# Regrouping the matrix work of a tuned attention and MLP block by tile mode, with a head that uses one PSUM bank per transposed chunk

## The chip, the cores and the metric

The kernel runs on one core of a Trainium2 chip. The metric is device time in microseconds (us) of one execution; less is better. "Span" is the length of the profiled execution, about 1.7 us less than the device time of the same run. A DMA is issued by an engine's queue and "lands" when its data have arrived. Engines: PE (matmul), DVE (vector), ACT (activation), POOL (GpSimd) and SP, which here only issues DMAs.

## The reference, cut to what matters

Sequence 2048, width 448, 16 heads of width 28, hidden width 1792; everything in bf16.

```python
xn = layernorm(x)
q, k, v = split(xn @ wqkv)                    # linear attention, phi(t) = t+1 or exp(t)
s = (phi(q) @ (phi(k).T @ v)) / (phi(q) @ sum(phi(k))) @ wo
g = silu(relu(xn @ w1 + b1)**2 @ w2 + b2)     # the gate
return x + s * g
```

The kernel splits the sequence into 16 tiles of 128 tokens. Its names for the stages are used below: H (xn @ w1, in groups of 512 tokens), K and Q, "q-rest" (the last 64 columns of q), token sum (xn.T @ phi(k)), den and spread (the denominator), gate (the product with w2, one per tile), S (phi(q) times the folded matrix). A tile's result is S x gate (a DVE instruction that reads S from PSUM), plus x (an "add", on POOL or DVE), and then one store.

Of the kernel before, what the change touches and what calls it, by code (L numbers as in the profile page):

```python
# [9 lines left out]
P = 128  # L10
# [5 lines left out]
NGB, NOB = 8, 6  # L16
# [12 lines left out]
class Op:  # L29
    def __init__(self, eng, emit, reads, writes, dur, alts, nbytes):  # L30
        self.eng, self.emit, self.dur, self.alts, self.nbytes = eng, emit, dur, alts, nbytes
        self.reads, self.writes = list(reads), list(writes)
        self.raw, self.deps, self.succ = set(), set(), []
        self.start = self.end = None
        self.seq = None
        self.late = 1e9
        self.prio = None
        self.sync = None
        self.fence = False
        self.fixed = 0.0  # L40
        self.hold = ()
        self.rank = None


class Program:
# [42 lines left out]
    def schedule(self):  # L88
# [26 lines left out]
        free["pool"] = 0.8  # L115
        dma_free = 0.0
# [31 lines left out]
        while n:  # L148
            best = None
            for e in self.ENGINES:  # L150
                if e in fixed:
# [17 lines left out]
                    cand = (st, 0, op, e, banks, op.dur)  # L169
# [37 lines left out]
            st, _, op, e, banks, du = best  # L207
            if op.eng != e:
                pend[op.eng].remove(op)
                op.eng = e  # L210
            else:
                pend[e].remove(op)
# [82 lines left out]
def bass_recurrent_scan__linear_attn_block__dense_activation_squared_relu__prompt_kernel(  # L295
    nc, A_x, A_wqkv, A_wo, B_x, B_w1, B_b1, B_w2, B_b2, out
):
    with ExitStack() as es:
# [205 lines left out]
        def pe_four(a, b, c, d, close=True, part=None, need=()):  # L504
# [10 lines left out]
            for lo, hi, us in ((0, 4, (a, c)), (4, 8, (b, d)), (8, 11, (c, a)), (11, 14, (d, b))):  # L515
# [18 lines left out]
                )  # L534
                ops.append(op)
# [6 lines left out]
        def pe_two(a, b, close=True):  # L542
            lo, hi, full = slice(0, 64), slice(64, 128), slice(0, 128)

            def f(e, _):
                for u in (a, b):
                    for k in range(3):
                        u[2](e, full, k, k == 0, False)
                a[2](e, lo, 3, False, close)
                return b[2](e, hi, 3, False, close)  # L550

            add("pe", f, a[1] + [r for r in b[1] if r not in a[1]], [a[0], b[0]], 7 * MM(a[4]) + 0.1)
            if close:
                a[3]()
                b[3]()

        def pe_main(u):
# [7 lines left out]
            add("pe", f, u[1], [u[0]], 3 * MM(u[4]) + 0.03)  # L565
# [16 lines left out]
        def pe_tails(a, b, close=True, need=()):  # L582
# [4 lines left out]
            op = add("pe", f, a[1] + [r for r in b[1] if r not in a[1]] + list(need) + [a[0], b[0]], [a[0], b[0]], MM(a[4]) + 0.1)  # L587
# [62 lines left out]
        def qx(u):  # L650
# [20 lines left out]
            add("pe", f, xnames(2 * u) + xnames(2 * u + 1) + wnames("wq") + ["wqh"], [b], 4 * MM(512) + 0.1)  # L671
# [45 lines left out]
        def dup(lo, hi, act=False):  # L717
            if act:
                add(
                    "act",  # L720
                    lambda e, _: e.activation(out=xn[:, lo:hi, D:512], in_=xn[:, lo:hi, 384:D], func=AF.Copy),
                    [("xn", k) for k in range(lo, hi)], [("xnd", k) for k in range(lo, hi)], 0.2,
                )
                return
            add(
                "dve", lambda e, _: e.tensor_copy(xn[:, lo:hi, D:512], xn[:, lo:hi, 384:D]),
                [("xn", k) for k in range(lo, hi)], [("xnd", k) for k in range(lo, hi)], 0.12,
            )

        def x_transpose0(lo, between=None):  # L730
            bs = [Buf("T"), Buf("T"), None, Buf("T")] if lo == 0 else [Buf("T")] * 4
            bs[2] = bs[0]

            def piece(cs, tail):
                def f(e, _):
                    last = None
                    for c in cs:
                        v = ps(bs[c])[:, :].bitcast(bf)
                        for k in (0, 1):
# [5 lines left out]
                    "pe", f, [(("xnd" if tail else "xn"), lo + k) for k in (0, 1)] + ["ident"],  # L745
                    list(dict.fromkeys(bs[c] for c in cs)), len(cs) * 0.114,
                )

            if lo == 0:
                piece((0, 1, 2), False)  # L750
                piece((3,), True)
            else:
                piece((0, 1, 2, 3), True)
            src = lambda c0, c1: (
                ps(bs[c0])[:, :].bitcast(bf)[:, c0 * 256 : c1 * 256].rearrange("p (c k t) -> p c k t", c=c1 - c0, k=2)
            )
            dst = lambda c0, c1: xT[:, lo : lo + 2, c0:c1, :].rearrange("p k c t -> p c k t")

            def on_act(c):
                return add(  # L760
                    "act", lambda e, _: e.activation(out=dst(c, c + 1), in_=src(c, c + 1), func=AF.Copy),
                    [bs[c]], [("xTp", lo, c)], 0.39,
                )

            def on_dve(c0, c1):
                return add(
                    "dve", lambda e, _: e.tensor_copy(dst(c0, c1), src(c0, c1)), [bs[c0]],
                    [("xTp", lo, c) for c in range(c0, c1)], 0.1 + 0.16 * (c1 - c0),
                )

            if lo == 0:
                on_act(0)
                on_dve(1, 2)
                on_act(2)
                between()
                return on_act(3)
            on_dve(0, 1)
            on_dve(1, 2)
            return on_dve(2, 4)

# [9 lines left out]
        def token_sum(c):  # L790
            b = Buf("A")

            def f(e, _):
# [14 lines left out]
            add(  # L808
                "pe", f, [(n, i) for n in ("pk", "xn") for i in range(NT)], [b], (16 if c < 3 else 8) * MM(D) + 0.1
            )  # L810
# [53 lines left out]
        def fold_wo(c):  # L864
# [15 lines left out]
            add("pe", f, ["kvd", "kvm", "wo"], [b], 0.19 * len(hs) + 0.05)  # L880
# [10 lines left out]
        def den():  # L891
            def f(e, _):
# [21 lines left out]
                [denb], 4 * 0.24,  # L914
            )
# [10 lines left out]
        def spread(c):  # L926
# [19 lines left out]
            add("pe", f, ["rden", "ehd"], bufs, 0.3)  # L946
# [69 lines left out]
        def gate(si, b, lo, hi, k, final):  # L1016
# [5 lines left out]
                "dve", lambda e, _: e.tensor_tensor(out=ob, in0=ps(b)[:, 0:w], in1=gs, op=ALU.mult),  # L1022
# [24 lines left out]

        def ss2(t, final=()):
            pe_two(*(sunit(si, si in final) for si in (t, t + 1)))

        def s_tails(parts):
# [4 lines left out]
            def f(e, _):  # L1056
                last = None
                for si, lo, hi, b in us:
                    r = slice(64 * (si % 2), 64 * (si % 2) + 64)
                    last = e.matmul(  # L1060
                        ps(b)[:, 0 : hi - lo], pqx[r, si // 8, (si % 8) // 2, :], msb[r, 3, lo:hi], start=True, stop=False
# [3 lines left out]
            add("pe", f, [("pqy", 3), ("msb", 3)], [u[3] for u in us], 0.2 * (len(us) // 2))  # L1065
            return us

        def s_main(u, k, final=True):
            si, lo, hi, b = u
            w = hi - lo  # L1070

            def f(e, _):
                last = None
                for c in range(3):
                    last = e.matmul(  # L1075
                        ps(b)[:, 0:w], pqT[:, c, si * P : (si + 1) * P], msb[:, c, lo:hi], start=False, stop=(c == 2)
# [39 lines left out]
        warm(40, 0.107)  # L1116
# [6 lines left out]
        dup(0, 1)  # L1123
        ln_rstd(1, 2)
        bias_columns()
        ln_norm(1)
        dup(1, 2, True)
        ln_stats(2)
        x_transpose0(0, lambda: ln_rstd(2, 3))
# [3 lines left out]
        dup(2, 3)  # L1133
        ln_norm(3)
        dup(3, 4)
        warm(4, 0.056)
# [3 lines left out]
        t23 = x_transpose0(2)  # L1140
# [27 lines left out]
        qx(0)  # L1168
        gg(0)
        gg(1)  # L1170
        ln(12, 16, lead=2)
# [3 lines left out]
        gg(2)  # L1175
        gg(3)
# [5 lines left out]
        quads("Q2.0 H3.4 Q2.1 H3.6 Q2.2 H3.5 Q3.0 H3.7 Q3.1 H3.12 Q3.2 H3.13")  # L1182
        qx(1)
        token_sum(0)
# [4 lines left out]
        token_sum(3)  # L1189
# [17 lines left out]
        ggs(6)  # L1207
        spread(3)
        ggs(7)
        ss4(0)  # L1210
        ggs(8)
        ggs(9)
        ss4(1)
        for si in range(10, 13):
            ggs(si)
        ss4(2)
        ggs(13)
        ggs(14)
        us = s_tails([(12, 0, D), (13, 0, D), (14, 0, D), (15, 0, 224), (15, 224, D)])
        for k in range(3):  # L1220
            s_main(us[k], k)
        gg_part(15, 0, 224)
        s_main(us[3], 3)
        gg_part(15, 224, D)
        s_main(us[4], 4)
# [30 lines left out]
```

## The kernel before: the parts that the change touches

448 is 3 x 128 + 64. A contraction over 448 is three full-array matmuls and one that fills only half of PE's rows; two such halves run side by side. A tile mode is the way in which PE's array is divided: used whole, or as row or column parts that work side by side; going from one to another is called a mode switch here. H, K, Q and S are written in a 64-row tile mode (two row halves at once), except for part of the first H work and the main part of the last S tiles, which use the full array; the gates use the full array; q-rests and the fourth token sum use a 64-column mode; spread uses a 32-row mode. PE writes its results to PSUM, which has eight banks. The main program is a list of such stages; a list scheduler in the kernel puts the instructions of the other engines in order, while PE keeps the order of the list.

```python
def x_transpose0(lo, between=None):           # head: tiles 0 and 1
    bs = [Buf("T"), Buf("T"), None, Buf("T")] if lo == 0 else [Buf("T")] * 4
    bs[2] = bs[0]                             # chunks 0 and 2 share a PSUM bank
    ...
    if lo == 0:
        piece((0, 1, 2), False)               # six transposes in one instruction group
        piece((3,), True)
    ...
# main program, cut
        quads("Q0.2 H1.12 Q1.0 H1.13"); qx(0); gg(0); gg(1)
        quads("K2.0 H2.0 ... H2.7"); gg(2); gg(3)
        ...
        qx(1); token_sum(0); token_sum(1); z_cols(); token_sum(2); den(); token_sum(3)
        quads("H3.8 H3.9 H3.10 H3.11")
        ...
        ggs(6); spread(3); ggs(7)
        ss4(0); ggs(8); ggs(9); ss4(1)
        for si in range(10, 13): ggs(si)
        ss4(2); ggs(13); ggs(14)
        us = s_tails([(12, 0, D), (13, 0, D), (14, 0, D), (15, 0, 224), (15, 224, D)])
        for k in range(3): s_main(us[k], k)   # adds of tiles 12, 13, 14 on DVE
        gg_part(15, 0, 224); s_main(us[3], 3)
        gg_part(15, 224, D); s_main(us[4], 4)
```

(`ss4(i)` is the S group of tiles 4i to 4i+3; its four adds run on POOL. Cuts are marked with dots; several calls are put on one line here.)

## Time and profile before

| | before |
|---|---|
| device time, median | 147.02 us (3 runs), 146.99 us in the 6 runs of the comparison |
| span of the profiled run | 145.4 us |
| PE busy | 141.2 us, 97% of the span |
| first H matmul | 6.81 us |
| last DVE add ends | 143.37 us (143.09 + 0.28) |
| last store issued | 143.39 us |

The page of the kernel before. The first line is the span, the second the busy time per engine with the number of instructions, the third the shares of the chain of waits, which is the chain of work that ended last:

```profile
span 145.4 us, 2861 instructions
...
PE 141.2 (97%) x1139; PEld 72.3 (50%) x1139; DVE 96.1 (66%) x219; ACT 79.5 (55%) x153; POOL 35.3 (24%) x51
...
PE 96%; DVE 1%; ACT 1%; issue 0%
```

PE is the bound: 96% of the chain is PE, and other engines' idle time costs nothing.

The chain of waits before, in order of time (start us, length us, what). L705 is the first H work, L709 H, L657 q-rest 0, L970 gates:

```profile
6.29 0.39 ACT xT L761
6.68 0.12 issue
6.81 2.12 PE pb L705 x18
...
11.79 1.09 PE pb L705 x9
...
14.82 0.86 PE pb L709 x8
...
37.49 0.98 PE pb L657 x8
38.47 5.40 PE pb L970 x28
...
96.29 2.65 PE pb L970 x14
...
100.82 2.75 PE pb L970 x14
...
143.09 0.28 DVE obuf L1028
```

A gate is 14 matmuls. After full-array work it takes 2.65 us; after another tile mode it takes 2.75 us. The first number gives 0.189 us for one matmul, so 28 should take 5.30 us and take 5.40. This 0.1 us per change of mode is what the change goes after.

The DMA view before, for the stretch in which the first 512 columns of w1 are issued (2.20 us); the last column is us from issue to landing:

```profile
w<-in_B_w_dram SPq DMA_DIRECT2D x1, 384.0 KB, 4.5
```

It lands at about 2.20 + 4.5 = 6.7 us, just when the copy (ACT, ends at 6.68) is done.

The end of the kernel before: from its timeline, POOL's adds for S group 2 and DVE's adds for tiles 12 to 14 (start us, us, engine, line, operation, count), and then SP's last two store issues, each asked for by itself:

```profile
132.08 4.00 POOL L1028 TENSOR_TENSOR obuf<-obuf,x_tok 128x448 bf16<-128x448 bf16 x4 [7.33 <-DVE obuf L1022]
...
139.65 0.98 DVE L1028 TENSOR_TENSOR obuf<-obuf,x_tok 128x448 bf16<-128x448 bf16 x3
...
141.66 0.33 SPq L401 DMA_DIRECT2D out_dram<-obuf  x1
...
143.39 0.33 SPq L401 DMA_DIRECT2D out_dram<-obuf  x1
```

POOL is done at 136.1 us, seven microseconds before the end. The last store is issued at 143.39 us, 0.02 us after its add.

### The profile page before, as it was taken

To read this page: it belongs to the slowest core of one execution; us is meant where nothing else is said; L and a number is where in the kernel's file an instruction comes from. 1 tells how busy PE (TensorE), PEld (TensorE's weight loads), DVE (VectorE), ACT (ScalarE), POOL (GpSimd) and SP (SyncE) were. 2 spreads that over 40 slices of the span, in tenths; PEclk is the share of its full clock that TensorE was granted. 3 is DMA by queue.
4 is the path that set the end of the run, shared out by engine and by line. 5 is a ranking of instruction groups with operands and counts; after the bars stand their busy time and mean duration, and the time that the engine had idled before them with its cause. 6 is when DMAs were issued, how large, how long until landed. Compare 5 with 4: busy or idle time off the path is not lost.

```text
span 145.4 us, 2861 instructions
## 1 busy us (share of the span) xinstructions
PE 141.2 (97%) x1139; PEld 72.3 (50%) x1139; DVE 96.1 (66%) x219; ACT 79.5 (55%) x153; POOL 35.3 (24%) x51
## 2 busy tenths in 40 slices
PE   7999999999999999999999999999999999999992
PEld 7884444444444444444443554454444544544481
DVE  6979888799987995278999500079683516216281
ACT  3627897988886981388879713897311110310300
POOL 2013026470000551630560000000000907306400
PEclk9999999999999999999999999999999999999999
DMA  4967699943301400000000000000000220200312
GB/s 90 316 231 227 146 247 371 330 110 72 77 0 34 111 5 0 0 0 5 0 2 0 5 0 0 0 2 5 0 0 0 66 65 32 95 0 5 126 62 64
DMA packets 16025, 10.53 MB, mean 72 GB/s; under 512 B 7500, under 2 KB 15628, under 8 KB 16012
## 3 DMA queue, kind: packets, MB, share of 16 engines
q1 hardware_dynamic: 15824, 10.28, 25.0%
q8 instruction: 9, 0.15, 0.4%
q10 hardware_dynamic: 188, 0.07, 0.2%
q14 instruction: 4, 0.03, 0.1%
HBM read 6.94 MB, written 1.84 MB: 60 GB/s over the span
## 4 chain that ended last, share of the span: by engine, by line
PE 96%; DVE 1%; ACT 1%; issue 0%
PE pb L970 28%; PE pb L709 26%; PE pb L617 7%; PE pb L797 6%; PE pb L643 6%; PE pb L1039 6%; PE pb L705 3%; PE pb L1089 3%; PE pb L992 2%; PE pb L1075 1%; PE pb L657 1%; PE pb L803 1%; PE pb L874 1%; PE pb L741 1%; PE pb L934 1%; PE pb L826 1%
## 5 line engine op out<-in xcount | busy, mean ns | idle before, releaser
L970 PE MATMUL pb<-w,r 128*128 128x448 bf16 x210 | 41.3, 353 | 0.0
L676 ACT ACTIVATE r<-pb,b1f 128x512 bf16<-128x512 f32 x54 | 33.8, 691 | 10.6 <-PE pb L709 10.6
L709 PE MATMUL pb<-xT,w 64*128 64x512 bf16 (+1 forms) x291 | 38.5, 376 | 0.0
L970 PEld LDWEIGHTS pb<-w,r 128*128 128x128 bf16 x210 | 19.8, 98 | 20.0 <-issue 1.5
L1012 ACT ACTIVATE gbuf<-gbuf 128x448 bf16<-128x448 bf16 x15 | 8.5, 581 | 29.7 <-DVE gbuf L979 29.7
L1028 POOL TENSOR_TENSOR obuf<-obuf,x_tok 128x448 bf16<-128x448 bf16 x12 | 12.0, 1032 | 48.6 <-DVE obuf L1022 48.6
L709 PEld LDWEIGHTS pb<-xT,w 64*128 64x128 bf16 (+1 forms) x291 | 14.1, 94 | 16.6 <-issue 0.4
L627 POOL TENSOR_TENSOR zacc<-zacc,pk 128x448 f32<-128x448 f32 x13 | 14.6, 1126 | 31.4 <-DVE pk L607 28.0
L979 DVE TENSOR_TENSOR gbuf<-pb,b2b 128x448 bf16<-128x448 f32 x15 | 9.4, 623 | 16.5 <-PE pb L970 16.4
L690 DVE TENSOR_TENSOR r<-r 128x512 bf16<-128x512 bf16 x35 | 16.8, 518 | 2.8 <-ACT r L676 2.7
L1022 DVE TENSOR_TENSOR obuf<-pb,gbuf 128x448 bf16<-128x448 f32 (+1 forms) x17 | 9.2, 592 | 6.6 <-PE pb L1039 4.7
L957 DVE TENSOR_TENSOR pqT<-pqT,pb 128x512 bf16<-128x512 bf16 x12 | 7.4, 681 | 8.8 <-PE pb L934 8.8
L617 PE MATMUL pb<-w_qkv,xT 64*128 64x448 bf16 x112 | 13.2, 349 | 0.0
L691 ACT ACTIVATE r<-r 128x512 bf16<-128x512 bf16 x21 | 12.6, 635 | 0.0
L643 PE MATMUL pb<-xT,w_qkv 64*128 64x512 bf16 x84 | 11.0, 376 | 0.0
L709 PE MATMUL pb<-xT,w_1r 64*128 64x512 bf16 x56 | 10.3, 377 | 0.0
L607 DVE SCALAR_TENSOR_TENSOR pk<-pb,pk 128x448 bf16<-128x448 f32 x16 | 9.9, 623 | 0.5
L461 DVE BATCH_NORM_STATS2 st<-x_tok 128x6 f32<-128x448 bf16 x16 | 9.2, 613 | 1.2 <-DMA x_tok<-in_A_x_dram 1.1
L595 ACT ACTIVATE pk<-pb 128x448 bf16<-128x448 f32 x16 | 7.8, 541 | 3.9 <-PE pb L617 3.9
L797 PE MATMUL pb<-pk,xn 128*128 128x448 bf16 x48 | 9.4, 353 | 0.0
L617 PEld LDWEIGHTS pb<-w_qkv,xT 64*128 64x128 bf16 x112 | 5.4, 94 | 6.1 <-issue 0.4
L607 DVE SCALAR_TENSOR_TENSOR pqT<-pb,pqT 128x512 bf16<-128x512 f32 x12 | 8.2, 690 | 0.3
(92 smaller groups left out, 133.7 us busy)
## 6 DMA issues: line engine op xcount, KB each, us to landing
out_dram<-obuf SPq DMA_DIRECT2D x15, 112.0 KB, 1.8
w<-in_B_w_dram SPq DMA_DIRECT2D x1, 1568.0 KB, 9.3
x_tok<-in_A_x_dram SPq DMA_DIRECT2D x3, 448.0 KB, 4.0
w<-in_B_w_dram SPq DMA_DIRECT2D x3, 384.0 KB, 4.5
w_qkv<-in_A_wqkv_dram SPq DMA_DIRECT2D x3, 336.0 KB, 5.7
w_o<-in_A_wo_dram SPq DMA_DIRECT2D x1, 392.0 KB, 9.1
w_qkv<-in_A_wqkv_dram SPq DMA_DIRECT2D x6, 56.0 KB, 5.2
x_tok<-in_A_x_dram SPq DMA_DIRECT2D x2, 112.0 KB, 2.1
```

Source lines behind the costliest of these rows:

```text
L607: lambda e, _: e.scalar_tensor_tensor(out=slot, in0=ps(buf)[:, 0:n], scalar=1.0 + 1e-6, in1=slot, op0=ALU.add, op1=ALU.max),
L617: return e.matmul(ps(b)[:, 0:D], xT[rw, si, c, :], w_qkv[rw, c, D : 2 * D], start=start, stop=stop)
L627: lambda e, _: e.tensor_tensor(out=o[:, 0:D], in0=pk[:, 0, :] if i == 1 else zacc[:, :], in1=pk[:, i, :], op=ALU.add),
L643: return e.matmul(ps(b)[:, 0:512], w_qkv[rw, c, m * P : (m + 1) * P], xT[rw, 4 * g : 4 * g + 4, c, :], start=start, stop=stop,)
L676: rl = lambda e, _: e.activation(out=slot, in_=ps(b)[:, 0:512], func=AF.Relu, bias=b1f[:, fi : fi + 1])
L690: return e.tensor_tensor(out=slot, in0=slot, in1=slot, op=ALU.mult)
L691: return e.activation(out=slot, in_=slot, func=AF.Square)
L709: return e.matmul(ps(b)[:, 0:512], lhs, xT[rw, 4 * g : 4 * g + 4, c, :], start=start, stop=stop, skip_group_check=not full,)
L797: last = e.matmul(ps(b)[:, 0:D], xn[:, si, c * P : (c + 1) * P], pk[:, si, :], start=(si == 0), stop=(si == NT - 1),)
L970: last = e.matmul(ps(b)[:, 0:D], r2[:, fi, si * P : (si + 1) * P], w_2[:, fi, :], start=(fi == 0), stop=(fi == NF - 1),)
L979: lambda e, _: e.tensor_tensor(out=gbuf[:, si % NGB, :], in0=ps(b)[:, 0:D], in1=b2b[:, :], op=ALU.add),
L1028: lambda e, _: e.tensor_tensor(out=ob, in0=ob, in1=x_tok[:, si, lo:hi], op=ALU.add),
```

## The change

The intent: put stages of the same tile mode next to each other, so that PE changes its mode less often; start H earlier with a PSUM bank per transposed chunk and with small copies moved to POOL. The core of the diff, cut:

```diff
-NGB, NOB = 8, 6
+NGB, NOB = 8, 8
 # head
-        def x_transpose0(lo, between=None):
-            bs = [Buf("T"), Buf("T"), None, Buf("T")] if lo == 0 else [Buf("T")] * 4
+        def x_transpose0(lo, pieces, share=()):
 ...
-        dup(0, 1)
+        dup(0, 1, "pool")
 ...
+        piece, evac = x_transpose0(0, [(0,), (1,), (2,), (3,)])
+        for c in range(4):
+            piece((c,))
+        evac("act", 0, 1)
 ...
 # middle
-        qx(0)
         gg(0)
         gg(1)
+        gg(2)
+        gg(3)
 ...
-        gg(2)
-        gg(3)
 ...
+        qx(0)
         qx(1)
+        token_sum(3)
         token_sum(0)
 ...
-        token_sum(3)
 # tail
         ggs(6)
+        ggs(7)
         spread(3)
-        ggs(7)
-        ss4(0)
-        ggs(8)
-        ggs(9)
+        ss4_rests_last(0)
         ss4(1)
-        for si in range(10, 13):
+        for si in range(8, 15):
             ggs(si)
         ss4(2)
-        ggs(13)
-        ggs(14)
-        us = s_tails([(12, 0, D), (13, 0, D), (14, 0, D), (15, 0, 224), (15, 224, D)])
+        us = s_tails([(12, 0, D), (13, 0, D), (14, 0, D), (15, 0, D)])
         for k in range(3):
-            s_main(us[k], k)
+            s_main(us[k], k, k > 0)
```

(The last line moves the add of tile 12 from DVE to POOL. `ss4_rests_last` is a new order inside S group 0 that leaves the half-array matmuls to the end. The cuts also leave out the scheduler's new cost of a mode switch.)

More of the change, by code (lines that the diff above doesn't have):

```diff
@@ L42, in __init__ @@
         self.rank = None
+        self.mode = "full"
 class Program:
@@ L115, in schedule @@
         free["pool"] = 0.8
+        mode = "full"
         dma_free = 0.0
@@ L168, in schedule @@
                     st = max(r, free[e])
-                    cand = (st, 0, op, e, banks, op.dur)
+                    switch = 0.1 if e == "pe" and op.mode != mode else 0.0
+                    cand = (st, 0, op, e, banks, op.dur + switch)
                 else:
@@ L207, in schedule @@
             st, _, op, e, banks, du = best
+            if e == "pe":
+                mode = op.mode
             if op.eng != e:
@@ L534, in pe_four @@
                 )
+                op.mode = "row64"
                 ops.append(op)
@@ L550, in f @@
                 return b[2](e, hi, 3, False, close)
-            add("pe", f, a[1] + [r for r in b[1] if r not in a[1]], [a[0], b[0]], 7 * MM(a[4]) + 0.1)
+            add("pe", f, a[1] + [r for r in b[1] if r not in a[1]], [a[0], b[0]], 7 * MM(a[4]) + 0.2)
             if close:
@@ L563, in f @@
                 return last
-            add("pe", f, u[1], [u[0]], 3 * MM(u[4]) + 0.03)
+            add("pe", f, u[1], [u[0]], 3 * MM(u[4]))
         def pe_part(us, part, cs=(0, 1, 2)):
@@ L585, in f @@
                 return b[2](e, slice(64, 128), 3, False, close)
-            op = add("pe", f, a[1] + [r for r in b[1] if r not in a[1]] + list(need) + [a[0], b[0]], [a[0], b[0]], MM(a[4]) + 0.1)
+            op = add("pe", f, a[1] + [r for r in b[1] if r not in a[1]] + list(need) + [a[0], b[0]], [a[0], b[0]], MM(a[4]))
+            op.mode = "row64"
             if close:
@@ L670, in qx @@
                 )
-            add("pe", f, xnames(2 * u) + xnames(2 * u + 1) + wnames("wq") + ["wqh"], [b], 4 * MM(512) + 0.1)
+            add("pe", f, xnames(2 * u) + xnames(2 * u + 1) + wnames("wq") + ["wqh"], [b], 4 * MM(512)).mode = "col64"
             phi(b, pqx[:, u, :, :].rearrange("p a b -> p (a b)"), ("pqx", u), 512)
@@ L715, in hh, with dup, piece @@
             return b, reads + w1names(fi // 4), mm, lambda: h_out(b, g, fi), 512
-        def dup(lo, hi, act=False):
-            if act:
-                add(
-                    "act",
-                    lambda e, _: e.activation(out=xn[:, lo:hi, D:512], in_=xn[:, lo:hi, 384:D], func=AF.Copy),
-                    [("xn", k) for k in range(lo, hi)], [("xnd", k) for k in range(lo, hi)], 0.2,
-                )
-                return
-            add(
-                "dve", lambda e, _: e.tensor_copy(xn[:, lo:hi, D:512], xn[:, lo:hi, 384:D]),
-                [("xn", k) for k in range(lo, hi)], [("xnd", k) for k in range(lo, hi)], 0.12,
-            )
-        def x_transpose0(lo, between=None):
-            bs = [Buf("T"), Buf("T"), None, Buf("T")] if lo == 0 else [Buf("T")] * 4
-            bs[2] = bs[0]
-            def piece(cs, tail):
+        def dup(lo, hi, eng="dve"):
+            add(
+                eng, lambda e, _: e.tensor_copy(xn[:, lo:hi, D:512], xn[:, lo:hi, 384:D]),
+                [("xn", k) for k in range(lo, hi)], [("xnd", k) for k in range(lo, hi)], 0.25 if eng == "pool" else 0.18,
+            )
+        def x_transpose0(lo, pieces, share=()):
+            bs = [None] * 4
+            for p in pieces:
+                b = Buf("T")
+                for c in p:
+                    bs[c] = b
+            for c, o in share:
+                bs[c] = bs[o]
+            def piece(cs, ks=(0, 1)):
                 def f(e, _):
@@ L738, in f @@
                         v = ps(bs[c])[:, :].bitcast(bf)
-                        for k in (0, 1):
+                        for k in ks:
                             o = (c * 2 + k) * P
@@ L744, in piece, with evac, f @@
                 add(
-                    "pe", f, [(("xnd" if tail else "xn"), lo + k) for k in (0, 1)] + ["ident"],
-                    list(dict.fromkeys(bs[c] for c in cs)), len(cs) * 0.114,
-                )
-            if lo == 0:
-                piece((0, 1, 2), False)
-                piece((3,), True)
-            else:
-                piece((0, 1, 2, 3), True)
-            src = lambda c0, c1: (
-                ps(bs[c0])[:, :].bitcast(bf)[:, c0 * 256 : c1 * 256].rearrange("p (c k t) -> p c k t", c=c1 - c0, k=2)
-            )
-            dst = lambda c0, c1: xT[:, lo : lo + 2, c0:c1, :].rearrange("p k c t -> p c k t")
-            def on_act(c):
-                return add(
-                    "act", lambda e, _: e.activation(out=dst(c, c + 1), in_=src(c, c + 1), func=AF.Copy),
-                    [bs[c]], [("xTp", lo, c)], 0.39,
-                )
-            def on_dve(c0, c1):
-                return add(
-                    "dve", lambda e, _: e.tensor_copy(dst(c0, c1), src(c0, c1)), [bs[c0]],
-                    [("xTp", lo, c) for c in range(c0, c1)], 0.1 + 0.16 * (c1 - c0),
-                )
-            if lo == 0:
-                on_act(0)
-                on_dve(1, 2)
-                on_act(2)
-                between()
-                return on_act(3)
-            on_dve(0, 1)
-            on_dve(1, 2)
-            return on_dve(2, 4)
+                    "pe", f, [(("xnd" if 3 in cs else "xn"), lo + k) for k in ks] + ["ident"],
+                    list(dict.fromkeys(bs[c] for c in cs)), len(cs) * len(ks) * 0.057,
+                )
+            def evac(eng, c0, c1):
+                def f(e, _):
+                    src = ps(bs[c0])[:, :].bitcast(bf)[:, c0 * 256 : c1 * 256].rearrange(
+                        "p (c k t) -> p c k t", c=c1 - c0, k=2
+                    )
+                    dst = xT[:, lo : lo + 2, c0:c1, :].rearrange("p k c t -> p c k t")
+                    if eng == "dve":
+                        return e.tensor_copy(dst, src)
+                    return e.activation(out=dst, in_=src, func=AF.Copy)
+                du = 0.37 * (c1 - c0) if eng == "act" else 0.1 + 0.18 * (c1 - c0)
+                return add(eng, f, [bs[c0]], [("xTp", lo, c) for c in range(c0, c1)], du)
+            return piece, evac
         def bias_columns():
@@ L806, in f @@
                 return last
-            add(
-                "pe", f, [(n, i) for n in ("pk", "xn") for i in range(NT)], [b], (16 if c < 3 else 8) * MM(D) + 0.1
-            )
+            op = add("pe", f, [(n, i) for n in ("pk", "xn") for i in range(NT)], [b], (16 if c < 3 else 8) * MM(D))
+            op.mode = "full" if c < 3 else "col64"
             def ev(e, eng):
@@ L878, in f @@
                 return last
-            add("pe", f, ["kvd", "kvm", "wo"], [b], 0.19 * len(hs) + 0.05)
+            add("pe", f, ["kvd", "kvm", "wo"], [b], 0.19 * len(hs) * (2 if c == 3 else 1))
             def ev(e, eng):
@@ L913, in den @@
                 + [("pqx", u) for u in (0, 1)],
-                [denb], 4 * 0.24,
-            )
+                [denb], 0.22,
+            ).mode = "col32"
             add(
@@ L944, in f @@
                 return last
-            add("pe", f, ["rden", "ehd"], bufs, 0.3)
+            add("pe", f, ["rden", "ehd"], bufs, 0.22).mode = "row32"
             for g in range(NG):
@@ L1021, in gate @@
             add(
-                "dve", lambda e, _: e.tensor_tensor(out=ob, in0=ps(b)[:, 0:w], in1=gs, op=ALU.mult),
+                "dve", lambda e, _: e.tensor_tensor(out=ob, in0=ps(b)[:, lo:hi], in1=gs, op=ALU.mult),
                 [b, ("gh", lo) if si == NT - 1 else ("g", si % NGB)], wr, 0.1 + w * 0.00118,
@@ L1046, in ss4, with ss4_rests_last, f @@
             pe_four(*(sunit(si, si in final) for si in (t, t + 2, t + 1, t + 3)))
+        def ss4_rests_last(i):
+            t = 4 * i
+            a, b, c, d = us = [sunit(si) for si in (t, t + 2, t + 1, t + 3)]
+            half = (slice(0, 64), slice(64, 128))
+            steps = ([], [])
+            for h in (0, 1):
+                first, second = ((a, b), (c, d))[:: 1 - 2 * h]
+                for u, s in ((first[0], True), (first[1], True), (second[0], False), (second[1], False)):
+                    steps[h].extend((u, k, s and k == 0, False) for k in range(3))
+                steps[h].extend((u, 3, False, True) for u in first)
+            ops = []
+            for lo, hi, pair in ((0, 3, (a, c)), (3, 6, (b, d)), (6, 9, (c, a)), (9, 12, (d, b)), (12, 13, (a, c)), (13, 14, (b, d))):
+                def f(e, _, lo=lo, hi=hi):
+                    last = None
+                    for j in range(lo, hi):
+                        for h in (0, 1):
+                            u, k, start, stop = steps[h][j]
+                            last = u[2](e, half[h], k, start, stop)
+                    return last
+                if lo < 12:
+                    reads = [("pq", i, k) for k in range(3)] + [("msb", k) for k in range(3)]
+                else:
+                    reads = [("pqy", i), ("msb", 3)]
+                banks = [u[0] for u in pair]
+                op = add("pe", f, reads + (banks if lo >= 6 else []), banks, (hi - lo) * MM(D))
+                op.mode = "row64"
+                ops.append(op)
+                if lo >= 6:
+                    op.sync = ops[-3]
+                if lo >= 12:
+                    for u in pair:
+                        u[3]()
         def ss2(t, final=()):
@@ L1060, in f, with s_main @@
                     last = e.matmul(
-                        ps(b)[:, 0 : hi - lo], pqx[r, si // 8, (si % 8) // 2, :], msb[r, 3, lo:hi], start=True, stop=False
-                    )
-                return last
-            add("pe", f, [("pqy", 3), ("msb", 3)], [u[3] for u in us], 0.2 * (len(us) // 2))
-            return us
-        def s_main(u, k, final=True):
-            si, lo, hi, b = u
+                        ps(b)[:, lo:hi], pqx[r, si // 8, (si % 8) // 2, :], msb[r, 3, lo:hi], start=True, stop=False,
+                        skip_group_check=True,
+                    )
+                return last
+            op = add("pe", f, [("pqy", 3), ("msb", 3)], [u[3] for u in us], 0.19 * ((len(us) + 1) // 2))
+            op.mode = "row64"
+            return us
+        def s_main(u, k, final=True, lo=0, hi=D):
+            si, b = u[0], u[3]
             w = hi - lo
@@ L1075, in f @@
                     last = e.matmul(
-                        ps(b)[:, 0:w], pqT[:, c, si * P : (si + 1) * P], msb[:, c, lo:hi], start=False, stop=(c == 2)
+                        ps(b)[:, lo:hi], pqT[:, c, si * P : (si + 1) * P], msb[:, c, lo:hi], start=False, stop=(c == 2),
+                        skip_group_check=True,
                     )
@@ L1114, in ln @@
             pr.lead = 0.0
-        warm(40, 0.107)
+        warm(36, 0.107)
         H0 = {fi: hh(0, fi, fi >= 7) for fi in range(NF)}
@@ L1122, in bass_recurrent_scan__linear_attn_block__dense_activation_squared_relu__prompt_kernel @@
         ln_norm(0)
-        dup(0, 1)
+        dup(0, 1, "pool")
         ln_rstd(1, 2)
         bias_columns()
+        warm(4, 0.107)
         ln_norm(1)
-        dup(1, 2, True)
+        dup(1, 2, "pool")
         ln_stats(2)
-        x_transpose0(0, lambda: ln_rstd(2, 3))
+        piece, evac = x_transpose0(0, [(0,), (1,), (2,), (3,)])
+        for c in range(4):
+            piece((c,))
+        evac("act", 0, 1)
+        evac("act", 1, 2)
+        ln_rstd(2, 3)
+        evac("dve", 2, 3)
+        evac("act", 3, 4)
         ln_stats(3)
@@ L1132, in bass_recurrent_scan__linear_attn_block__dense_activation_squared_relu__prompt_kernel @@
         ln_norm(2)
-        dup(2, 3)
+        dup(2, 3, "pool")
         ln_norm(3)
         dup(3, 4)
-        warm(4, 0.056)
         for c in range(3):
@@ L1139, in bass_recurrent_scan__linear_attn_block__dense_activation_squared_relu__prompt_kernel @@
         pe_part([H0[i] for i in range(4, 6)], 0)
-        t23 = x_transpose0(2)
+        piece, evac = x_transpose0(2, [(0, 1, 2, 3)])
+        piece((0, 1, 2, 3), (0,))
+        piece((0, 1, 2, 3), (1,))
+        evac("dve", 0, 1)
+        evac("dve", 1, 2)
+        t23 = evac("dve", 2, 4)
         pr.hot = None
@@ L1207, in bass_recurrent_scan__linear_attn_block__dense_activation_squared_relu__prompt_kernel @@
         ggs(6)
+        ggs(7)
         spread(3)
-        ggs(7)
-        ss4(0)
-        ggs(8)
-        ggs(9)
+        ss4_rests_last(0)
         ss4(1)
-        for si in range(10, 13):
+        for si in range(8, 15):
             ggs(si)
         ss4(2)
-        ggs(13)
-        ggs(14)
-        us = s_tails([(12, 0, D), (13, 0, D), (14, 0, D), (15, 0, 224), (15, 224, D)])
+        us = s_tails([(12, 0, D), (13, 0, D), (14, 0, D), (15, 0, D)])
         for k in range(3):
-            s_main(us[k], k)
+            s_main(us[k], k, k > 0)
         gg_part(15, 0, 224)
-        s_main(us[3], 3)
+        s_main(us[3], 3, True, 0, 224)
         gg_part(15, 224, D)
-        s_main(us[4], 4)
+        s_main(us[3], 4, True, 224, D)
         pr.schedule()
```

## The prediction

> **What bounds the kernel now.** The page gives a span of 145.4 us for a 147.02 us time. PE is busy 97% of the span, and the chain of waits is 96% PE and 0% issue; the longest waits belong to other engines. So only shorter PE work, or PE idle time at the two ends, counts.
>
> **Mode switches.** In the chain, stretches of one tile mode cost more than their matmuls only after a change of mode. Warm 448-column matmuls follow each other every 0.189 us. The two first-gate groups (28 matmuls = 5.30 us) show 5.40 us after a 64-row or 64-column stretch; the gate group that follows full-array work shows 2.65 us for 14, others 2.75; the first q-rest stretch shows 0.98 us against 0.86 us. A switch thus costs 0.10 to 0.12 us. The Trainium skill, "TensorEngine Tiling (Array Packing)", section Key Properties, says that changing the tiling mode drains TensorE; the trace agrees, with about 0.105 us each.
>
> I counted switches in the PE order of both kernels: 31 before, 22 after. Removed: one because q-rest 0 no longer interrupts gate/H work; two because gates 0-3 stand together; one because both q-rests and the 64-column token sum are adjacent; one by gates 6 and 7 together; four by two S groups directly after spread 3, seven gates in a row, and S group 2 next to the tails. 9 x 0.105 = 0.95 us, all on PE and so all on the chain. The tail of tile 15 as one 448-column matmul instead of two halves saves nothing: it already ran beside tile 14's.
>
> **Head.** Before, the first H matmul starts at 6.81 us, after a copy (ends 6.68) that waited for six transposes because two chunks share a bank. One bank per chunk lets this copy end near 6.2 us (estimate: cold transposes take 0.108 us, the copy 0.39 us). But the DMA view gives the first w1 block as issued at 2.20 us with 4.5 us to landing, so it lands near 6.7 us, and the load order does not change. I expect the start to move by only 0.05 to 0.1 us, not 0.5. The second set of transposes already followed matmuls without a gap; moving the small copies to POOL gives no more there. The short gap before 9.77 us stays.
>
> **Risks, costed.** Spread 3 (four banks), gate 7's bank and S group 0 (four banks) want nine of eight: up to 0.2 us. Without gates 2 and 3 in the middle, about 27 us of H/K/Q run unbroken; per K+H pair PE needs 1.42 us, ACT 1.23, DVE about 1.31, so I expect little stall. The last outputs crowd into the final 6 us, where POOL adds (1.03 us each) must finish before the last tile; I think they do. I charge 0.05 to 0.2 us for all this.
>
> **Prediction.** 147.02 - 0.95 - 0.07 (head) + 0.1 = 146.1 us, range 145.6 to 146.5. Chances: faster by over 2% 0.02, within 2% 0.96, slower by over 2% 0.02.
>
> **What would show it.** Right: gates 0-3 in one stretch of about 10.7 us, the seven gates of about 18.65 us, two S groups about 5.4 us in a stretch; PE busy falls by about 1 us with the matmul count nearly unchanged; first H matmul near 6.75 us, now released by the w1 DMA. Wrong: first H matmul near 6.3 us (the head is worth 0.5 us more, about 145.6), or new PE idle time at the S groups, in the H/K/Q stretch, or a later last output.
>
> **What would make it wrong.** Landing of the first w1 block misread; a stall on banks or on the DVE queue; the contention of POOL and DVE at the end.

## The result, and the profile after

The changed kernel took 146.74 us (median of 6 runs, 146.72 to 146.83), the kernel before 146.99 us (6 runs). The ratio is 0.9981, with a 95% interval of 0.9968 to 0.9994. A ratio is always the mean time of one kernel's fast runs over that of the other's of the same rounds, so it is not quite the ratio of the medians. The gain is 0.25 us where 0.9 was predicted, and 146.74 lies above the stated range.

The page after:

```profile
span 145.1 us, 2851 instructions
...
PE 140.2 (97%) x1134; PEld 72.5 (50%) x1134; DVE 95.7 (66%) x218; ACT 78.2 (54%) x150; POOL 36.5 (25%) x55
...
PE 96%; DVE 1%; ACT 1%; issue 0%
```

PE's busy time fell by 1.0 us, and the chain's shares are the same. (The chain ends with the last add. The last store comes after it, so this view cannot show what happens to that store.) Yet the span fell by only 0.3 us. The chain of waits after (L712 first H work, L716 H, L957 gates, L1026 S groups):

```profile
6.04 0.39 ACT xT L762
6.43 0.10 issue
6.54 2.13 PE pb L712 x18
...
11.51 1.09 PE pb L712 x9
...
14.54 1.01 PE pb L716 x8
...
37.36 10.70 PE pb L957 x56
...
108.96 5.45 PE pb L1026 x56
114.42 18.64 PE pb L957 x98
...
142.02 0.28 DVE obuf L1015
```

Gates 0 to 3 are one stretch of 10.70 us, the seven late gates one of 18.64 us, and two S groups one of 5.45 us; all three numbers were in the prediction (10.7, 18.65, 5.4). The first H matmul comes 0.27 us earlier, but at 14.54 us eight matmuls that take 0.86 us elsewhere take 1.01. The last add ends at 142.30 us, 1.07 us earlier than before (143.37). So on the compute engines the change did a little more than predicted. The missing time lies after the last add: from there to the end of the span it is 145.4 - 143.37 = 2.03 us before and 145.1 - 142.30 = 2.80 us after, 0.77 us longer. (Spans are given to 0.1 us, so such a difference is good to about 0.05 us.)

The end of the changed kernel, from its timeline, and then SP's last five stores in their order, each asked for by itself:

```profile
135.99 5.14 POOL L1015 TENSOR_TENSOR obuf<-obuf,x_tok 128x448 bf16<-128x448 bf16 x5 [15.76 <-DVE obuf L1009]
...
139.02 1.23 DVE L1015 TENSOR_TENSOR obuf<-obuf,x_tok 128x448 bf16<-128x448 bf16 x1
...
142.02 0.28 DVE L1015 TENSOR_TENSOR obuf<-obuf,x_tok 128x224 bf16<-128x224 bf16 x1
...
141.16 0.33 SPq L406 DMA_DIRECT2D out_dram<-obuf  x1
...
141.53 0.43 SPq L406 DMA_DIRECT2D out_dram<-obuf  x1
...
142.01 0.44 SPq L406 DMA_DIRECT2D out_dram<-obuf  x1
...
142.49 0.45 SPq L406 DMA_DIRECT2D out_dram<-obuf  x1
...
142.99 0.45 SPq L406 DMA_DIRECT2D out_dram<-obuf  x1
```

Read it from the top. S group 2 now stands just before the tail, and tile 12's add went to POOL as well, so POOL adds without a pause until 135.99 + 5.14 = 141.13 us. SP issues the stores in one fixed order. Tile 12's store is ahead of those of 13, 14 and the two halves of 15; it goes out at 141.16, as soon as POOL is done. Tile 13, ready since 139.02 + 1.23 = 140.25 us, had to wait behind it. From there five issues follow each other every 0.37 to 0.50 us, and the last one starts at 142.99 us although its data have been ready since 142.30. That is 0.69 us of lateness, where the kernel before had 0.02. The last store also landed 1.6 us after its issue instead of 1.5; the four stores ahead of it took 1.7 to 1.8 us, where the last five of the kernel before took 1.5 to 1.8.

Two theories fit this. **Issue queue:** the last store is late because SP's fixed order holds it behind a late POOL add. **Traffic:** too many bytes are written in the last microseconds, so that stores are slow whatever their order. A third possibility is that the mode switches are worth less than they look. The experiments tell these apart; a second set looks at the head.

### The profile page after: what moved, and what is told of

It is laid out like the page before. It is cut to its first block, busy times and chain, and to the rows that moved or that the text cites. A ratio compares the mean times of both kernels' runs of the same rounds, so it can differ in the third digit from the quotient of the medians.

```text
span 145.1 us, 2851 instructions
## 1 busy us (share of the span) xinstructions
PE 140.2 (97%) x1134; PEld 72.5 (50%) x1134; DVE 95.7 (66%) x218; ACT 78.2 (54%) x150; POOL 36.5 (25%) x55
## 4 chain that ended last, share of the span: by engine, by line
PE 96%; DVE 1%; ACT 1%; issue 0%
PE pb L957 28%; PE pb L716 26%; PE pb L624 7%; PE pb L785 6%; PE pb L650 6%; PE pb L1026 6%; PE pb L712 3%; PE pb L1114 3%; PE pb L979 2%; PE pb L1099 1%; PE pb L664 1%; PE pb L861 1%; PE pb L791 1%; PE pb L921 1%; PE pb L813 1%; PE pb L883 1%
## 5 line engine op out<-in xcount | busy, mean ns | idle before, releaser
L957 PE MATMUL pb<-w,r 128*128 128x448 bf16 x210 | 40.6, 353 | 0.0
L716 PE MATMUL pb<-xT,w 64*128 64x512 bf16 (+1 forms) x291 | 38.3, 376 | 0.0
L957 PEld LDWEIGHTS pb<-w,r 128*128 128x128 bf16 x210 | 20.2, 98 | 19.5 <-issue 1.2
L1015 POOL TENSOR_TENSOR obuf<-obuf,x_tok 128x448 bf16<-128x448 bf16 x13 | 13.1, 1043 | 53.9 <-DVE obuf L1009 53.9
L716 PEld LDWEIGHTS pb<-xT,w 64*128 64x128 bf16 (+1 forms) x291 | 14.2, 94 | 16.5 <-ACT r L683 0.4
L697 DVE TENSOR_TENSOR r<-r 128x512 bf16<-128x512 bf16 x37 | 17.4, 502 | 2.0 <-ACT r L683 1.9
L698 ACT ACTIVATE r<-r 128x512 bf16<-128x512 bf16 x19 | 11.2, 633 | 0.0
L716 PE MATMUL pb<-xT,w_1r 64*128 64x512 bf16 x56 | 10.3, 377 | 0.0
L607 DVE TENSOR_SCALAR pk<-pk 128x448 bf16<-128x448 bf16 x16 | 6.0, 377 | 4.3 <-ACT pk L602 4.2
```

The lines of the kernel that those rows point to most:

```text
L697: return e.tensor_tensor(out=slot, in0=slot, in1=slot, op=ALU.mult)
L698: return e.activation(out=slot, in_=slot, func=AF.Square)
L716: return e.matmul(ps(b)[:, 0:512], lhs, xT[rw, 4 * g : 4 * g + 4, c, :], start=start, stop=stop, skip_group_check=not full,)
L957: last = e.matmul(ps(b)[:, 0:D], r2[:, fi, si * P : (si + 1) * P], w_2[:, fi, :], start=(fi == 0), stop=(fi == NF - 1),)
L1015: lambda e, _: e.tensor_tensor(out=ob, in0=ob, in1=x_tok[:, si, lo:hi], op=ALU.add),
```

## The experiments

A note on size: the times of the kernel before scatter more on some chips (146.9 to 148.5 us in the first set below) than in the comparison above, so the traces are compared too. The trace measure used is the length from the start of the nine-matmul stretch of the head (about 11.8 us before) to the end of the last add, which leaves the start of the kernel out.

### e1: tile 12's add back on DVE

```diff
-            s_main(us[k], k, k > 0)
+            s_main(us[k], k)
```

> The changed kernel with one edit: the residual add of tile 12 goes to DVE instead of POOL. Theory (issue queue): SP issues the output stores in a fixed order; in the changed kernel tile 12's store waits for the fifth POOL add (ends 141.13 us), and four stores that follow it, issued about 0.45 us apart, push the last one to 143.0 us though its data are ready at 142.30. Without the fifth POOL add the last store should be issued within 0.1 us of the last DVE add, and the time should fall by 0.6 to 0.7 us to about 146.1 us. Rival (traffic): the last stores land late because too many bytes are written at the end; the bytes and the span they are written in hardly change, so the time should stay near 146.7 us. Second point, for both: DVE adds with two SBUF inputs that run beside POOL adds should last until the POOL add ends (over 0.6 us instead of 0.34).

Measured: 146.41 us, before 147.24 us on the same chip, ratio 0.9932 (0.9899 to 0.9964). The timeline of e1, with POOL's and DVE's adds and SP's last store:

```profile
136.14 4.00 POOL L1015 TENSOR_TENSOR obuf<-obuf,x_tok 128x448 bf16<-128x448 bf16 x4 [15.76 <-DVE obuf L1009]
...
139.16 1.23 DVE L1015 TENSOR_TENSOR obuf<-obuf,x_tok 128x448 bf16<-128x448 bf16 x1
...
142.48 0.44 SPq L406 DMA_DIRECT2D out_dram<-obuf  x1
```

The last add ends at 142.44 us and the last store starts at 142.48. With nothing changed but one add of 1 us on another engine, the lateness is gone, although the same stores leave as close together: SP starts the last five at 140.54, 141.02, 141.50, 141.98 and 142.48 us, which is the row of the changed kernel (141.16 to 142.99) 0.5 to 0.6 us earlier. So e1 escapes only just: its queue has no time to spare. From the last add to the end of the span it is 144.6 - 142.44 = 2.16 us instead of 2.80. The issue-queue theory holds. The last store took 1.6 us to land, against 1.5 before; this and the issue together leave 0.13 us over the kernel before, about all that crowded stores can be charged with.

The 1.23 us of the DVE add is a second matter. It ends at 140.39 us, 0.25 us after POOL's last add (140.14). See e8.

### e2: only the last store issued from ACT's queue

```diff
-            dma("sp", tok(out, si, si + 1)[:, 0, lo:hi], ob, [("out", si, lo)], P * w * 2, [nm])
+            dma("act" if k == 4 else "sp", tok(out, si, si + 1)[:, 0, lo:hi], ob, [("out", si, lo)], P * w * 2, [nm])
```

(A second small edit keeps the scheduler's order of everything else as it was.)

> The changed kernel with one edit: the very last store (second half of tile 15) is issued by ACT's queue instead of SP's. Issue-queue theory: it is issued at about 142.35 us, right after its add; the store before it, still on SP, is issued at about 142.5 us and lands near 144.2, so the time falls by about 0.4 us to 146.35 us. Traffic rival: the same bytes now crowd more closely, landing takes longer, the time stays within 0.1 us of 146.74.

Measured: 146.7 us, ratio 0.9948 (0.9917 to 0.998). ACT issued the last store at 142.45 us, and the store before it left SP at 142.61. From the last add (142.42) to the end it is 145.0 - 142.42 = 2.58 us: 0.22 us better than the changed kernel, about half of what was expected, while the last two stores now land side by side, 1.8 us after issue, where the last one took 1.6. The time of 146.7 us is what the traffic rival had forecast, so e2 shows that another queue issues the last store on time, but it does not part the two theories; e1 does. The Trainium skill, "DMA: Bandwidth & Descriptors", section "Issuing engines are not separate DMA queues", says that a second issuing engine saves only the sequencer's time to start a DMA, "which is usually small relative to the DMA itself". This case agrees on what is saved, but at the end of a kernel it is not small: the issue of a store takes 0.33 to 0.46 us and a store lands in 1.5 to 1.9 us.

### e3: S group 2 ahead of gates 13 and 14 again

```diff
-        for si in range(8, 15):
+        for si in range(8, 13):
             ggs(si)
         ss4(2)
+        ggs(13)
+        ggs(14)
```

> The changed kernel with one part undone: S group 2 stands before gates 13 and 14 again, as in the kernel before, so that its four POOL adds and stores are out of the way of the tail. Costs two tile-mode switches (0.21 us). Issue-queue theory and traffic rival both expect the late 0.7 us to vanish: 146.74 + 0.21 - 0.7 = 146.25 us, last store issued within 0.1 us of the last add. If the tail loss has another cause, such as the nine switches being worth less than they look, the time rises to about 146.95.

Measured: 146.2 us, ratio 0.9923 (0.989 to 0.9955). The last add ends at 142.76 us, the last store starts at 142.79, and 144.8 - 142.76 = 2.04 us follow. Two more switches than in the changed kernel, and still faster: the tail cost more than those switches save.

### e4: the middle of the change alone

```diff
 # the kernel before, with only:
-        qx(0)
         gg(0)
         gg(1)
+        gg(2)
+        gg(3)
 ...
+        qx(0)
         qx(1)
+        token_sum(3)
```

> The kernel before with only the middle of the change: gates 0 to 3 together, both q-rests and the 64-column token sum together. Removes 4 of the 31 tile-mode switches and leaves the head and the tail as they were. Switch theory: 4 x 0.105 = 0.42 us less, 146.57 us against 146.99. Rival (the saved switches come back as waits on PSUM banks or on DVE and ACT in the unbroken H/K/Q stretch): 146.85 us or more, with new idle time of PE.

Measured: 146.89 us, before 147.24 us, ratio 0.9964 (0.9929 to 0.9999). The time is 0.35 us under before on the medians, near the expected 0.42, and the interval is wide; the 146.89 us itself would fit the rival, but the kernel before was slower on this chip too. The trace settles the size of a switch:

| kernel | switches | nine-matmul stretch to last add | less than before |
|---|---|---|---|
| before | 31 | 143.37 - 11.79 = 131.58 us | |
| e4 | 27 | 143.30 - 12.11 = 131.19 us | 0.39 us |
| e3 | 24 | 142.76 - 11.92 = 130.84 us | 0.74 us |
| e2 | 22 | 142.42 - 11.78 = 130.64 us | 0.94 us |
| e1 | 22 | 142.44 - 11.80 = 130.64 us | 0.94 us |
| changed | 22 | 142.30 - 11.51 = 130.79 us | 0.79 us, with the 0.15 us lost at 14.54 us |

Four, seven and nine removed switches give 0.39, 0.74 and 0.94 us: 0.10 us each, with nothing given back in the long H/K/Q stretch. The idea that switches are worth less than they look falls.

### e5: the head alone

The kernel before with the changed head and the old middle and tail. (It was made from the changed kernel, so the scheduler's switch cost and the eight output buffers stay.)

> The kernel before with only the head of the change (one bank per transposed chunk, copies to POOL, order of the head). Load theory: in most executions the first H matmul waits for the first w1 block (runs so far show it released by that load at 6.80 and 7.13 us, and at 6.54 us by the copy when the load came early), so the head is worth 0 to 0.2 us: 146.8 to 147.0 us where before has 146.99, ratio 0.9985 to 1.000. Rival (the transposes and copies alone set the start): 0.3 to 0.5 us less, ratio about 0.997.

Measured: 147.08 us, before 147.22 us, ratio 0.9996 (0.9976 to 1.0016). So the time shows no gain from the head; the interval could still hide about 0.3 us either way. Its chain of waits shows why:

```profile
4.78 5.78 DMA x_tok<-in_A_x_dram
10.56 0.02 issue
10.58 2.21 DVE st L466 x4
...
13.10 0.30 ACT vep L475
...
13.64 1.16 ACT r L683 x2
14.80 0.05 issue
14.85 1.04 PE pb L716 x8
```

The first H matmul came at 6.70 us, but at 14.85 us PE waits for PSUM banks that ACT has to free. ACT takes its instructions in order; ahead of those relus stands the reciprocal root of the layer norm of tiles 4 to 7, whose input is the load of these tiles, issued at 4.78 us and landed at 10.56. In this run an earlier start only made PE wait longer there.

### e6 and e7: the first w1 block in three loads, with the new head and with the old one

```diff
 # e6: on e1; e7: on the kernel before
+            if p == 0:
+                for c in range(3):
+                    dma(eng, w_1[:, c, lo:hi], B_w1[c * P : (c + 1) * P, lo:hi],
+                        [("w1", p, 0, c)], 256 * (hi - lo), reads)
```

> The kernel of e1 with the first w1 block loaded as three 128 KB pieces (one per 128 rows), each waited for by itself, so that the first H matmul needs a third of the bytes. Load theory: the first H matmul now starts at 6.5 to 6.6 us, released by the ACT copy in every run; the second w1 block, issued about 0.8 us later, may become the next wait. Time 0.1 to 0.4 us under e1. Rival (the load does not limit): same time as e1, ratio about 0.994.

> The kernel before with the same split of the first w1 block and its old head. Load theory: the first H matmul starts at 6.8 us, released by the copy that waited for six transposes; so with the load out of the way the new head is worth 0.25 us at that point (6.8 against 6.55). Time within 0.3 us of before. Rival: no difference between old and new head.

Measured: e6 147.15 us, ratio 0.9995 (0.9976 to 1.0013), where e1's ratio was 0.9932; e7 147.79 us, ratio 1.0046 (1.0028 to 1.0064). Both are misses as improvements. The first H work of e6 (from PE's timeline):

```profile
6.33 1.13 PE L722 MATMUL pb<-xT,w 128*128 128x256 bf16 x8
7.71 0.60 PE L722 MATMUL pb<-xT,w 128*128 128x256 bf16 x4 [0.24 <-DMA w<-in_B_w_dram]
8.70 0.83 PE L722 MATMUL pb<-xT,w 128*128 128x256 bf16 x6 [0.39 <-DMA w<-in_B_w_dram]
```

The start came somewhat earlier than expected (6.5 to 6.6), at 6.33 us against 6.86 with the old head in e7, so with the load out of the way the new head starts 0.5 us earlier. But the next two stretches wait for loads: two more issues delay every later load by about 0.9 us, among them that of tiles 4 to 7, which heads e7's chain at 5.69 us instead of 4.78. The earlier start was lost again to loads. That the load decides also shows without this edit: the unsplit first block took 4.0 us to land in e1, 4.2 in the changed kernel, 4.5 before and 4.8 in e4, and in e4 and e2 the first H matmul was released by it, at 7.13 and 6.80 us.

### e8: no POOL work in the tail

```diff
 # on e1
-        ss4(2)
+        ss4(2, (8, 9, 10, 11))       # the four adds of S group 2 on DVE
```

> The kernel of e1 with all four residual adds of S group 2 on DVE too, so that POOL does nothing in the last 7 us. Port theory: the DVE add that lasted 1.23 us beside a POOL add in the changed kernel, e1 and e2 lasts 0.34 us, like every other. Rival (the add is long for another reason, such as its place in the queue): still over 0.6 us. The time itself may be worse, since DVE has four more adds in its queue before the last one.

One look: 148.15 us, state unknown, worse as the text above allows, because adds stand in DVE's queue behind the last tile. The question was how long one add takes. The tile view of the output buffer, min/median/max in ns:

```profile
L1015 DVE TENSOR_TENSOR obuf<-obuf,x_tok x6: 381/382/385, 139.1 to 142.3; 128x448 bf16<-128x448 bf16 x6
```

Without POOL beside it the same add takes 0.38 us instead of 1.23. The Trainium skill, "SBUF — State Buffer", section "SBUF: two separate sides", says that VectorE and GpSimd share a port pair under an exclusive lock, held for a whole instruction, which a VectorE instruction with two SBUF inputs needs when the GpSimd one reads SBUF. The DVE add and the POOL add both have two SBUF inputs, and the traces agree: in e1 the DVE add ended 0.25 us after POOL's, and in the changed kernel those of tiles 13 and 14 (1.23 and 0.91 us long) ended at 140.25 and 141.38 us, each 0.25 us after a POOL add (140.00 and 141.13). The product before it, which reads S from PSUM, kept its usual 0.62 us beside POOL. This did not set the time of the changed kernel, though: e1 has the same 1.23 us and no late store.

### e9, e10 and e11: a better order of the tail, the control, and a try at the head

e9 moves gates 13 and 14 between the last S tiles. Those are full-array work like the gates, so no switch is added, and S group 2 with its POOL adds gets 5.3 us of room:

```diff
-        for si in range(8, 15):
+        for si in range(8, 13):
             ggs(si)
         ss4(2)
         us = s_tails([(12, 0, D), (13, 0, D), (14, 0, D), (15, 0, D)])
-        for k in range(3):
-            s_main(us[k], k, k > 0)
+        s_main(us[0], 0, False)
+        ggs(13)
+        s_main(us[1], 1)
+        ggs(14)
+        s_main(us[2], 2)
```

> The changed kernel with gates 13 and 14 moved behind the tails and between the last S tiles: S group 2 and the tails still share one 64-row stretch and the gates and last S tiles are all full-array, so there are 22 tile-mode switches as in the changed kernel, but POOL has 5.3 us more for its five adds. Issue-queue theory: PE stretch as short as in e1 and e2, last store issued within 0.1 us of the last add, store landing back at about 1.5 us, no DVE add longer than 0.5 us; 0.6 to 0.8 us under the changed kernel run on the same chip, and about 0.1 to 0.2 us better than e1 and e3 were against before (ratio about 0.992). Rival (bank or gate waits appear because four S banks stay open longer): less than 0.4 us under the changed kernel.

> The changed kernel unaltered, as a control on the chip of e9: 146.6 to 147.0 us, last store issued about 0.7 us after its data are ready, ratio about 0.998 as before.

Measured on one chip: before 147.1 us, the changed kernel 146.71 (146.65 to 146.75), e9 146.0 (145.79 to 146.21); ratios to before 0.9978 for the changed kernel and 0.9929 (0.9917 to 0.9942) for e9. e9 beats both kernels in every run. Its timeline, with POOL's adds, the last full DVE add and SP's last store:

```profile
130.88 4.99 POOL L1015 TENSOR_TENSOR obuf<-obuf,x_tok 128x448 bf16<-128x448 bf16 x5 [10.46 <-DVE obuf L1009]
...
139.59 0.39 DVE L1015 TENSOR_TENSOR obuf<-obuf,x_tok 128x448 bf16<-128x448 bf16 x1
...
142.50 0.33 SPq L406 DMA_DIRECT2D out_dram<-obuf  x1
```

POOL is done at 135.9 us, the add takes 0.39 us, the last add ends at 142.47 and the store starts at once; 144.5 - 142.47 = 2.03 us follow, as before. The control repeated the late store: 142.80 us against an add that ended at 142.09. It repeated the stretch of the table above too: 142.09 - 11.40 = 130.69 us, 0.89 less than before, with only 0.06 us lost at 14.43 us; there the load of tiles 4 to 7 took 5.1 us to land instead of the 5.4 of the changed kernel's first profile.

In e9's profile PE stood idle for 0.32 us until 14.70 us, for the reason found in e5. e11 is e9 with `lead=0` instead of `lead=3` for the layer norm of tiles 4 to 7.

> The kernel of e9 with a smaller lead for layer norm of tiles 4 to 7, which puts their reciprocal-root step on ACT behind four relus instead of two. Theory for the head: ACT runs in order, this step waits for the x tiles 4 to 7 to land (10.2 to 10.6 us) and be reduced, and the relus behind it hold the PSUM banks that PE wants at 14.5 us. With the step later the wait of about 0.15 us (up to 0.5 us when that load is late) at that point is gone, and the time falls by 0.1 to 0.3 us. Rival: the transposed tiles 4 to 7 then come too late for the first K1 matmul at 22.6 us, and PE waits there instead.

Measured: 147.26 us, ratio 1.0011 (0.9998 to 1.0024), worse than e9. Its chain:

```profile
14.37 0.86 PE pb L716 x8
...
21.17 2.88 DMA xT<-xn
24.05 0.05 issue
24.10 1.04 PE pb L716 x8
```

The time did not fall. What the theory said of the wait and what the rival said of the tiles both came true: the wait at 14.4 us is gone (0.86 us again), so it was indeed ACT's order that caused it; but the transposed tiles 4 to 7 arrive only at 24.05 us, and PE waits for them, as the rival said. It is not their load that is late here (issued at 4.76 us, 5.1 us to landing): the layer norm now stands behind other work of ACT and DVE, and the transposing DMA begins only at 21.17 us. So neither order is free: with `lead=3` the relus wait for the layer norm, and with `lead=0` the layer norm waits for other work.

## Why the prediction was wrong, point by point

- **PE bounds the kernel, and a switch of tile mode costs about 0.105 us: right.** 31 - 22 = 9 switches, predicted 0.95 us, measured 0.94 us (e1, e2), with 0.74 for seven and 0.39 for four. The Trainium skill, "TensorEngine Tiling (Array Packing)", section Key Properties, gives the reason (a drain) but no size.
- **The head brings 0.05 to 0.1 us, not 0.5: near in its size, partly by luck.** The prediction had the first H matmul near 6.75 us, released by the first w1 load. That load does decide the start in some runs (e2, e4). In the changed kernel's profiled run it landed early, the copy released PE at 6.54 us, and 0.15 of the 0.27 us gained was lost at 14.54 us, a wait that the prediction did not name. That the net 0.12 us is near the predicted 0.07 comes from two misses that cancel. Alone the head gave 0.9996 (e5), too coarse to tell 0.12 us from nothing. What I did not see is the load of tiles 4 to 7, which takes part of the gain back, or all of it, depending on when it lands.
- **Risks in the long H/K/Q stretch and on the banks at S group 0: harmless, as predicted.** The two S groups took 5.45 us for 5.40.
- **The tail: this step failed.** The prediction said that POOL adds "must finish before the last tile; I think they do", and charged "0.05 to 0.2 us for all this". They do finish, at 141.13 us against 142.30. That was the wrong question. What counts is when SP may issue the last store, and SP issues in a fixed order, with tile 12's store, which waits for the fifth POOL add, ahead of four others that then need 0.37 to 0.50 us each. The term was 0.77 us (2.80 - 2.03): 0.67 us of a later issue and about 0.1 us of slower landing. e1 and e9 remove it without touching a switch; e2 removes a part. The contention of POOL and DVE, which the prediction named as a risk, did come (two adds of 1.23 and 0.91 us instead of 0.38), but it was not what made the store late.

The sum on the profiled runs: -0.94 (switches) - 0.12 (head, net) + 0.77 (tail) = -0.29 us, and the spans differ by -0.3 us.

## What to carry to other kernels

Count tile-mode switches in PE's order, and price them by the same stretch with and without a switch before it: here 0.10 us each, and grouping paid in full. When regrouping moves work toward the end, follow the last tiles past the compute engines to the queue that issues their stores: here the stores of a queue went out in program order, each took 0.33 to 0.46 us to issue, and one that waited for a slow engine held all behind it. If work has to move, look for a place of the same tile mode that keeps the slow consumer away from the end, as in e9.

## What the Trainium skill lacked or had wrong

- "TensorEngine Tiling (Array Packing)" says that a change of tiling mode drains TensorE, without a size: 0.10 us per switch here, 0.39, 0.74 and 0.94 us for four, seven and nine of them.
- "DMA: Bandwidth & Descriptors" calls the issue time usually small: it was 0.33 us alone and 0.43 to 0.45 us in a row, and five stores in a row made the last one 0.69 us late. What it lacks is a warning that a store which waits for its data holds back the stores behind it in the same queue, so that the order of issue becomes a dependency of its own at the end of a kernel.
- No page read for this case gives the scatter of a load's landing at the start of a kernel: the same 384 KB load, issued at the same time, took 4.0 to 4.8 us to land in different runs, more than the head of the change could gain.
- "SBUF — State Buffer" was right on the shared port (0.38 us alone, 1.23 us beside POOL).
